# Where the remainder tiles of cosine attention stand, in what order norms and loads come, and how the first weights are split

## The chip, the cores and the metric

The kernel runs on one core of a Trainium2 chip. The metric is the device time of one execution in microseconds (us); shown are a median of three runs and one profiled execution.

## What is computed

Inputs are q, k and v of 8 batches, 12 heads, 448 tokens and 64 elements in f32, the scalar tau, and two weights, `w_in` (768 x 2048) and `w_out` (2048 x 768). The reference, cut:

```python
q_n = q / (norm(q, axis=-1) + 1e-06);  k_n = k / (norm(k, axis=-1) + 1e-06)
attn = softmax(q_n @ k_n.T / tau)              # per batch and head
x = (attn @ v).transpose(0, 2, 1, 3).reshape(8 * 448, 768)
h = x @ w_in
out = maximum(0.01 * h, h) @ w_out             # 3584 x 768, f32
```

## The kernel before

**Attention by pairs of heads.** The 12 heads of a batch make 6 pairs, 48 pairs in all; pair s is pair s % 6 of batch s // 6. `load_qk` (L134) brings a pair's q and k by four DMAs on SyncE's queue into one of six slots of `raw_sb`. `squares` (L170) squares them on GpSimd, `sums` (L183) sums over the 64 elements on VectorE, `roots` (L194) takes the root by Ln and Exp on ScalarE, and `normalise` (L210) divides on VectorE, which gives `qn`. `transposes` (L245) turns `qn` into `qkT`: for pairs 0 to 9 on TensorE and with a copy on VectorE, from pair 10 on (`DMA_FROM`) by one DMA transpose on SyncE's queue. `norm` (L689) is roots, normalise and transposes of one pair, then loads of a later pair, a one-element copy on GpSimd that waits for this pair's `qn` (`hold`, L508), and the squares of a later pair behind it. `ss`, `qn` and `sq` have three buffers each, `qkT` five.

**Scores.** 448 tokens are three key tiles of 128 and a rest of 64. `key_tiles` (L264) computes a tile of keys against all 448 queries of both heads of a pair (L276: two matmuls of 64 rows side by side), then Exp on ScalarE (L288). The rests of two pairs share one remainder tile (ki = 3): eight matmuls in a 64 x 64 arrangement for two tiles, four for one. A batch has 18 key tiles and 3 remainder tiles. `attend_two` and `attend` (L660, L649) form the totals and products with v (L303 for the rests, L316 for the others), the reciprocals on ScalarE (L335, L336) and the scaled result `xT` on VectorE (L357).

**The two matrix products.** Tokens are taken in chunks, by turns of 384 and 512 columns, chunk b with batch b. `first` (L371) computes 128 rows m of h for a chunk: six matmuls over kt (L380), then the leaky ReLU on ScalarE (L387). `firsts` (L707) does all 16 m of a chunk and calls, ahead of given m, the functions of a table (`between`). `groups` (L438) computes one row of 128 tokens of the output in two halves, as 32 steps of two 64-row matmuls side by side (L455), and yields after each step. At the half of a row TensorE waits until the two halves' products have drained. `second` (L406) does the last chunk's rows (L417).

**A visit.** `visit` (L717) goes through the rows of chunk b and lays the 18 key tiles of batch b+1 between their steps: a table says after which steps, one or two at a time (`three` for rows of 384 columns, `four` for 512, `wide` for the first visit, where two rows go together). Two remainder tiles stand at the beginning (L722), the third at the end (L732). `norms` tells which norms of later pairs are called after which steps. Then `attend_batch` (L678), v's loads on GpSimd's queue, and `firsts` of the next chunk. There are seven visits, 0 to 6. All order is written out by hand, engine by engine; each engine runs its instructions in the order in which they are written.

**Banks.** The eight PSUM banks are dealt by `banks` (L75): the ones that were dealt or given back longest ago; a pair of banks for a key tile and for a row of `groups`, one for an m of `first`.

**The beginning.** Before the first visit, batch 0's attention runs pair by pair (`scaled`, L566, and `bulk`, L552, set the loads of v, w_in and further pairs), then the first m of chunk 0. `load_w_in` (L103) loads, by GpSimd's queue, one of four quarters: half of the 2048 columns, and the even or the odd kt. `load_w_out` (L109) loads a quarter of w_out, four m.

## Time and profile before

| | |
|---|---|
| median of three runs | 410.41 us (409.35 to 410.95) |
| profiled execution | 409.29 us, span 407.5 us |
| TensorE (PE) busy | 399.5 us, 98% |
| ScalarE (ACT) busy | 263.0 us, 65% |
| VectorE (DVE) busy | 189.1 us, 46% |
| GpSimd (POOL) busy | 139.5 us, 34% |
| stretch from the start to the first visit | 51.2 us |
| visits 0 and 1 begin at | 51.2 and 98.8 us |

Busy time of TensorE counts matmuls that overlap in its pipeline once; how full it is inside that time is read from the starts of neighbouring instructions. Lines of the views below give start and length in us, engine, line, operation, tiles, shape and count, and in brackets the idle time before and what ended it. A name such as `64*128` behind the tiles is the part of TensorE's array that a matmul takes.

### The profile page before, as it was taken

What the parts mean: (1) busy time and instruction counts of PE and PEld (TensorE: products, weight loads), DVE (VectorE), ACT (ScalarE), POOL (GpSimd) and SP (SyncE); (2) the same over time, 40 slices, a digit from 0 to 9 for tenths busy, and PEclk for the clock granted to TensorE, in tenths of its full rate; (3) what the DMA queues carried; (4) which work ended last, traced back from release to release, by engine and by line L of the source; (5) the groups of instructions that cost most, each with busy time, mean ns of one, the idle gap of its engine ahead of it and who ended that gap; (6) DMA issues with size and microseconds to landing.
All of it is one profiled execution on the core that took longest, in us unless ns stands there. A gap on an engine that the chain in (4) does not pass through costs nothing.

```text
span 407.5 us, 10174 instructions
## 1 busy us (share of the span) xinstructions
PE 399.5 (98%) x4086; PEld 215.8 (53%) x4096; DVE 189.1 (46%) x405; ACT 263.0 (65%) x454; POOL 139.5 (34%) x213
## 2 busy tenths in 40 slices
PE   8889999999999999999999999999999999999996
PEld 3335666544555655544555555544555555554564
DVE  6986941771644624354542635256261645130021
ACT  4996588565865688745876569845876559944300
POOL 4973661571323522253241614055231530000000
PEclk9999999999999999999999999999999999999999
DMA  7999999694496859378384947485478742210033
GB/s 187 252 209 235 194 184 213 196 209 107 117 204 101 146 83 218 63 119 179 78 207 103 137 114 165 110 117 138 93 183 151 103 82 63 63 41 2 0 78 78
DMA packets 102095, 54.21 MB, mean 133 GB/s; under 512 B 69984, under 2 KB 96992, under 8 KB 102048
## 3 DMA queue, kind: packets, MB, share of 16 engines
q1 hardware_dynamic: 78064, 41.04, 43.8%
q0 software_dynamic: 23136, 12.00, 22.5%
q8 instruction: 32, 0.52, 0.5%
q10 hardware_dynamic: 848, 0.52, 0.4%
q14 instruction: 15, 0.12, 0.1%
HBM read 45.61 MB, written 11.01 MB: 139 GB/s over the span
## 4 chain that ended last, share of the span: by engine, by line
PE 87%; DMA 8%; POOL 3%; DVE 1%; issue 0%; ACT 0%; POOLq 0%
PE ps L380 32%; PE ps L455 31%; PE ps L316 10%; PE ps L276 7%; DMA raw_sb<-in_k_dram 5%; PE ps L417 5%; DMA w_in_sb<-in_moe_w_in_dram 2%; POOL sq L179 1%; PE ps L303 1%; POOL v_rem L164 1%; DVE qn L219 0%; POOL v_b L157 0%; POOL raw_sb L129 0%; POOL w_in_sb L105 0%; ACT L65 0%
## 5 line engine op out<-in xcount | busy, mean ns | idle before, releaser
L380 PE MATMUL ps<-xT,w_in_sb 128*128 128x384 bf16 (+1 forms) x760 | 147.8, 352 | 1.0 <-DMA w_in_sb<-in_moe_w_in_dram 0.6
L455 PE MATMUL ps<-w_out_sb,hT 64*128 64x384 bf16 x1536 | 143.5, 323 | 0.0
L288 ACT ACTIVATE pe<-ps 128x896 bf16<-128x896 f32 x144 | 123.6, 918 | 19.9 <-PE ps L276 18.0
L387 ACT ACTIVATE hT<-ps 128x384 bf16<-128x384 f32 (+1 forms) x128 | 67.6, 543 | 71.7 <-PE ps L380 71.3
L380 PEld LDWEIGHTS <-w_in_sb 128*128 128x128 bf16 x768 | 74.1, 98 | 72.4 <-issue 4.0
L455 PEld LDWEIGHTS <-hT 64*128 64x128 bf16 x1536 | 75.0, 94 | 53.9 <-PE ps L455 4.2
L179 POOL TENSOR_TENSOR sq<-raw_sb 128x512 f32<-128x512 f32 x92 | 84.9, 943 | 17.2 <-DMA raw_sb<-in_k_dram 16.3
L219 DVE TENSOR_TENSOR qn<-raw_sb,r 128x512 bf16<-128x512 f32 x96 | 58.0, 646 | 1.9 <-DVE r L215 0.3
L276 PE MATMUL ps<-qkT 64*128 64x448 bf16 (+1 forms) x384 | 55.0, 354 | 1.6 <-DVE qkT L257 0.8
L467 DVE COPY osb<-ps 128x384 f32<-128x384 f32 x41 | 21.2, 553 | 74.0 <-PE ps L455 43.6
L190 DVE TENSOR_REDUCE ss<-sq 128x6 f32<-128x384 f32 (+1 forms) x95 | 54.4, 610 | 1.2 <-POOL sq L179 1.0
L510 POOL CAST seen<-qn 128x1 f32<-128x1 bf16 x47 | 8.7, 186 | 122.0 <-DVE qn L219 121.1
L214 DVE TENSOR_SCALAR ss<-ss 128x14 f32<-128x14 f32 x48 | 9.5, 197 | 69.4 <-ACT ss L198 69.3
L357 DVE TENSOR_TENSOR xT<-ps,rb 128x448 bf16<-128x448 f32 x48 | 27.8, 620 | 27.2 <-ACT rb L336 27.1
L157 POOL DMA_DIRECT2D v_b<-in_v_dram x24 | 18.6, 777 | 54.2 <-PE ps L316 54.2
L316 PE MATMUL ps<-pe,v_b 128*32 128x448 bf16 x576 | 32.0, 353 | 0.0
L276 PEld LDWEIGHTS <-qkT 64*128 64x128 bf16 (+1 forms) x384 | 16.7, 96 | 20.6 <-issue 8.7
L423 DVE COPY osb<-ps 128x384 f32<-128x384 f32 (+1 forms) x9 | 4.6, 513 | 36.6 <-issue 22.6
L316 PEld LDWEIGHTS <-v_b 128*32 128x32 bf16 x576 | 15.1, 97 | 12.0 <-issue 0.6
L288 ACT ACTIVATE pr<-ps 128x896 bf16<-128x896 f32 x24 | 21.3, 920 | 0.2 <-PE ps L276 0.2
L335 ACT ACTIVATE rb<-ps 128x448 f32<-128x448 f32 x24 | 12.9, 537 | 13.1 <-PE ps L316 12.2
L417 PE MATMUL ps<-w_out_sb,hT 128*128 128x384 bf16 (+1 forms) x144 | 21.0, 308 | 0.0
(48 smaller groups left out, 185.0 us busy)
## 6 DMA issues: line engine op xcount, KB each, us to landing
raw_sb<-in_q_dram SPq DMA_DIRECT2D x48, 192.0 KB, 3.6
raw_sb<-in_k_dram SPq DMA_DIRECT2D x46, 192.0 KB, 3.8
out_dram<-osb SPq DMA_DIRECT2D x30, 192.0 KB, 2.8
v_b<-in_v_dram POOLq DMA_DIRECT2D x24, 192.0 KB, 4.8
out_dram<-osb SPq DMA_DIRECT2D x12, 384.0 KB, 3.2
w_in_sb<-in_moe_w_in_dram POOLq DMA_DIRECT2D x4, 768.0 KB, 13.2
w_out_sb<-in_moe_w_out_dram POOLq DMA_DIRECT2D x4, 768.0 KB, 9.6
raw_sb<-in_q_dram SPq DMA_DIRECT2D x43, 32.0 KB, 3.5
```

What stands on the lines that cost most here:

```text
L179: eng.tensor_tensor(sq, x, x, op=ALU.mult)
L190: nc.vector.tensor_reduce(o.rearrange("p (h t) -> p h t", h=2), sqs[s][i], axis=AX.X, op=ALU.add)
L219: scalings[s] = nc.vector.tensor_tensor(qn[s][:, lo:hi], x.rearrange("p h t d -> p t h d"), r[:, r0 : r0 + 2 * nt].rearrange("p (h t) -> p ...
L276: nc.tensor.matmul(out=out[:, a, :S], lhsT=x[rows, c0:c1], rhs=x[rows, 0:S], start=True, stop=True,)
L288: nc.scalar.activation(out=dst, in_=sc[:, :, :S], func=AF.Exp, scale=inv_tau)
L316: nc.tensor.matmul(out=x[32 * g : 32 * g + 32, :S], lhsT=weights(g, ki) if ki < 3 else rem(g), rhs=pe[s][:, ki, a, :] if ki < 3 else pr[j] ...
L357: scalings[j, e] = nc.vector.tensor_tensor(xT[m][:, 2 * jj + e, half * S : (half + 1) * S], pos.pop((j, e))[:, :S], rbs[j], op=ALU.mult,)
L380: nc.tensor.matmul(out=pm[:, :n], lhsT=w_in_sb[:, kt, m * 128 : (m + 1) * 128], rhs=xT[c // 2][:, kt, c0 : c0 + n], start=(kt == 0), stop= ...
L387: nc.scalar.activation(out=hT[c][:, m, :n], in_=pms.pop((c, m))[:, :n], func=AF.Prelu, alpha=0.01)
L417: nc.tensor.matmul(out=po2[:, :n], lhsT=hT[c][:, m, ts * 128 : (ts + 1) * 128], rhs=w_out_sb[:, m, lo : lo + n], start=(m == 0), stop=(m = ...
L455: done[p][i] = nc.tensor.matmul(out=pos2[p][:, i, :HALF], lhsT=hT[c][rows, m, ts * 128 : (ts + 1) * 128], rhs=w_out_sb[rows, m, half * HAL ...
L467: copy(out=osb[c, ts][:, half * HALF : (half + 1) * HALF], in_=po2[:, i, :HALF])
```

## The change

It has four parts. In visits 1 to 6 all three remainder tiles stand at the visit's beginning, and the key tiles' steps are set anew; in visit 0 the last row gets two key tiles at its half and one step less. Pairs are normed earlier, so that all six of a batch are turned before their visit begins; in `firsts` of the odd chunks the norms follow one another without loads, and the loads come together behind them (pairs 12 to 17 behind norm 11); `qkT` gets seven buffers. Around the first visit, pairs 8 to 11 are loaded, squared and normed earlier, and the w_out quarters follow norms 6 to 8. The first half of w_in's columns is loaded in three parts of two neighbouring kt each instead of two parts of three; its second half is loaded as before, both parts at one place.

```diff
-    qtp = ctx.enter_context(tc.tile_pool(name="qt", bufs=5))
+    qtp = ctx.enter_context(tc.tile_pool(name="qt", bufs=7))
...
-    def load_w_in(i):
-        n0, e = i // 2 * (D_ff // 2), i % 2
...
+    def load_w_in(half, j=slice(None), e=slice(None)):
+        n = slice(half * D_ff // 2, (half + 1) * D_ff // 2)
+        gp.dma_start(out=w_in_t[:, j, e, n], in_=w_in_r[:, j, e, n])
...
         if s == 0:
             load_v(1)
-            load_w_in(0)
+            load_w_in(0, j=0)
         elif s == 1:
             load_v_rem(0, slice(2, 4))
-            load_w_in(1)
+            load_w_in(0, j=1)
         elif s == 2:
+            load_w_in(0, j=2)
             load_v(2)
-            load_w_in(2)
         elif s == 3:
-            load_w_in(3)
+            for e in range(2):
+                load_w_in(1, e=e)
...
-        if s in (0, 2):
-            load_qk(7 + s // 2)
+        if s == 0:
+            load_qk(7)
+        elif s == 2:
+            load_qk(8)
+            load_qk(9)
         elif s == 4:
             behind(nc.sync, scalings[5], "weights first")
-            load_qk(9)
+            load_qk(10)
...
+        if s == 4:
+            squares(8)
...
     def attend_batch(b):
         if b == 1:
-            load_qk(14)
-            load_qk(15)
             sums(12)
         attend_two(b * NQ)
-        if b == 1:
-            norm(12)
+        if b % 2:
+            norm(12 if b == 1 else (b + 1) * NPAIR + 1)
...
-    def norm(s, transposed=True):
+    def norm(s, transposed=True, load=True):
...
-        for x in (12, 13) if s == 11 else (s + 4,) if s > 11 else ():
+        for x in range(12, 18) if s == 11 else (s + NPAIR,) if s > 11 and load else ():
             load_qk(x)
...
-        squares(s + 2)
-        if s in (7, 8):
-            load_w_out((4,) if s == 7 else (8, 12))
+        if s not in (9, 17):
+            squares(s + (3 if s < 9 else 2))
+        if s < 9:
+            load_w_out((4 * (s - 5),))
...
-        key_tiles([(s0 + 1, 3), (s0 + 3, 3)])
+        key_tiles([(s0 + 1, 3), (s0 + 3, 3)] + [(s0 + 5, 3)] * (b > 0))
...
-        key_tiles([(s0 + 5, 3)])
+        if b == 0:
+            key_tiles([(s0 + 5, 3)])
...
+    wide = (at(5, 11, 16, 22, 27, 33, 38, 44, 49, 55, 60), at(4, 8, 12, 16, 16, 21, 26))
+    three = (at(9, 16, 16, 21, 26, 31), at(5, 10, 16, 16, 21, 26, 31), at(5, 10, 16, 16, 20))
+    four = (at(9, 16, 16, 24), at(4, 10, 16, 16, 24), at(4, 10, 16, 16, 24), at(5, 10, 16, 16))
...
-            5: [lambda: sums(8), lambda: transposes(6)],
-            7: [lambda: norm(8, False), lambda: transposes(7)],
-            8: [lambda: sums(9)],
-            10: [lambda: norm(9, False), lambda: load_v(3)],
-            11: [lambda: transposes(8), lambda: load_v(4)],
-            13: [lambda: load_v(5), lambda: load_v_rem(1)],
-            14: [lambda: transposes(9), lambda: sums(10)],
+            4: [lambda: norm(8, False)],
+            5: [lambda: transposes(6), lambda: sums(9)],
+            7: [lambda: transposes(7)],
+            8: [lambda: norm(9, False)],
+            10: [lambda: transposes(8), lambda: load_v(3)],
+            11: [lambda: sums(10), lambda: load_v(4)],
+            12: [lambda: transposes(9)],
+            13: [lambda: norm(10), lambda: load_v(5), lambda: load_v_rem(1)],
+            15: [lambda: sums(11)],
...
+        s = (b + 2) * NPAIR
+        if b == 0:
+            norms = {(0, 3): [lambda: norm(11)]}
+        elif b % 2:
             norms = {}
+            for i in range(3):
+                norms[i, 4] = [lambda x=s + i: norm(x)]
+                norms[i, 20] = [lambda x=s + i + 1: sums(x)]
+        else:
+            norms = {(2, 8): [lambda: sums(s + 1)], (2, 22): [lambda: norm(s)]}
...
+        if b % 2:
             between = {
+                0: [lambda: norm(s + 3)], 2: [lambda: sums(s + 4)], 4: [lambda: norm(s + 4)],
+                6: [lambda: sums(s + 5)], 8: [lambda: norm(s + 5)], 12: [lambda: sums(s + 6)],
             }
         else:
+            left = range(s + (2 if b else 1), s + NPAIR)
+            between = {}
+            for x, m in zip(left, (0, 3, 5, 8, 10)):
+                between[m] = [lambda x=x: sums(x), lambda x=x: norm(x, load=False)]
+            between[12] = [lambda x=x: load_qk(x + NPAIR) for x in left]
+            if b == 0:
+                between[12].append(lambda: squares(19))
+            between[14] = [lambda: sums(s + NPAIR)]
```

## The prediction

> **What bounds the kernel now.** I read the page first (busy times, chain), then the instructions of TensorE in order of time, then those of VectorE, GpSimd and SyncE's queue around the places that the edits touch.
>
> ```profile
> span 407.5 us, 10174 instructions
> ...
> PE 87%; DMA 8%; POOL 3%; DVE 1%; issue 0%; ACT 0%; POOLq 0%
> ```
>
> The profiled execution took 409.29 us, its span 407.5; 1.8 us lie around it. The chain that ends last is TensorE's for 87%; the DMA and GpSimd pieces of it all lie before 49 us. So from there on an edit counts only through what it takes out of TensorE's stream or puts in as a wait. In order of time (start, length, engine, line, tiles; the stretch is the visit of chunk 1 with its beginning and end):
>
> ```profile
> 98.84 0.57 PE L276 MATMUL ps<-qkT 64*64 64x448 bf16 x8
> 99.34 0.99 PE L455 MATMUL ps<-w_out_sb,hT 64*128 64x384 bf16 x10
> 100.17 0.35 PE L276 MATMUL ps<-qkT 64*128 64x448 bf16 x2
> 100.35 1.14 PE L455 MATMUL ps<-w_out_sb,hT 64*128 64x384 bf16 x12
> ...
> 120.96 2.76 PE L455 MATMUL ps<-w_out_sb,hT 64*128 64x384 bf16 x32
> 123.65 0.38 PE L276 MATMUL ps<-qkT 64*64 64x448 bf16 x4
> 123.96 0.38 PE L303 MATMUL ps<-pr,ones 64*32 64x448 bf16 x8
> ```
>
> Read starts against starts. Twelve L455 matmuls last 0.98 us (one pair 0.1625), a key tile (L276, 64*128) between them 0.18 to 0.19, and neither leaves a gap: the spreading of the key tiles costs nothing. Only the remainder tiles (L276, 64*64) do: two of them at the beginning take 0.50 for two rounds of 0.19, so 0.12 is a switch of shape; one at the end takes 0.31, again 0.19 and 0.12, and 0.09 before it (120.96 and 16 x 0.1625 is 123.56).
>
> Small losses before that, in the same view:
>
> ```profile
> 29.46 0.34 PE L380 MATMUL ps<-xT,w_in_sb 128*128 128x384 bf16 x1
> 30.38 0.66 PE L380 MATMUL ps<-xT,w_in_sb 128*128 128x384 bf16 x3 [0.59 <-DMA w_in_sb<-in_moe_w_in_dram]
> ...
> 48.54 0.79 PE L233 MATMUL ps<-id,qn 128*128 128x128 bf16 x7
> 49.16 2.11 PE L380 MATMUL ps<-xT,w_in_sb 128*128 128x384 bf16 x12
> ...
> 67.50 0.37 PE L276 MATMUL ps<-qkT 64*128 64x448 bf16 x2
> 67.84 0.83 PE L455 MATMUL ps<-w_out_sb,hT 64*128 64x384 bf16 x8
> ```
>
> First, the second product of w_in waits for the load with the odd kt: 0.92 from start to start instead of 0.16, so 0.76. Second, the transposes of pair 9 take 0.62 instead of the 0.39 of the other pairs (they wait for the norm): 0.23. Third, one key tile at the half of a row takes 0.34 instead of 0.19: 0.15.
>
> **The change part by part**
>
> *w_in by quads.* One load of 512 KB now brings kt 0 and 1, where two of 768 KB did. The four loads of before landed at 24.4, 30.4, 37.4 and 41.8 us (issue and time to landing, load by load). As the queue is backlogged, bytes count: kt 0 and 1 are there by about 22, kt 2 and 3 by 27, kt 4 and 5, after the same bytes as the second load, at 30.4, needed at 35. So -0.76. GpSimd issues five loads instead of four, 0.77 us more, with idle time behind. But the last quarter still lands at 41.8 at the earliest, and its first use, the second matmul of m=8, stands at 42.47, so at 41.7 after the gain. The loads of pairs 9 and 10, now issued 7 to 9 us earlier, share the DMA engines with it and can cost 0.6 more. I give back 0.35 of bounds 0 and 0.76: **-0.4**.
>
> *Norms of pairs 8 to 11 earlier.* Pair 9 was late because its sums ran at 44.69, behind the scaling of pair 8; that norm moves from m=7 to 4, pair 9's from 10 to 8, and their transposes from 11 and 14 to 10 and 12. If pair 9's load, issued 7 us earlier, lands some 2 us earlier than its 41.25, squares and sums follow by 42 and the transposes, at about 45.8, wait no more: **-0.23**; if it lands no earlier, scaling ends at 46.2, +0.2. The w_out load of m 12 to 15 is now behind squares(11): issued at about 52 instead of 50.3, landed 10.0 later in a queue that is full until 60.3; it is needed at 61.2 before and at 60.4 now: +0.1 (0 to 0.6).
>
> *Visit 0.* The last row gets its doubled key tile at the half: **-0.15** (0 at the least, as another stall may take its place).
>
> *Remainder tiles.* In visits 1 to 6 the third stands behind the first two. It costs one round, 0.19, there; at the end 0.31 + 0.09 go, and the direct change from L455 (64*128) to L303 (64*32), which no row shows, comes: between 0 and 0.19 (the change from 64*32 to 128*32 at 124.16, where 16 matmuls of two rounds take 0.57). With the 0.09 that stands before the 64*64 tile: -0.12 a visit, **-0.7** for six (0 to -1.3). [...] All eight banks are now dealt at a visit's beginning: the first row's pair falls to the banks of m=14 and 15, whose L387 runs from 98.94 to 99.54 and would end about when the row starts, at 99.53. I take +0.1 for the three visits after chunks of 512, none for 384. The key tiles that follow (n=9, 16, 16, 21 ...) find their banks free by 0.3 to 0.8 us, with one exp of 0.8 to 0.86 after the other on ScalarE; ScalarE does 21 of them, 17.9 us, in a visit of 19.9.
>
> *The price: all six pairs turned before the visit.* The third remainder tile needs pair s+5's DMA transpose at the visit's beginning. In the even visits after a chunk of 384 the last norm stands at m=8, as one does now: its transpose was issued at 141.49, 3.4 us to landing, so 144.9, needed at 146.6. In visits 3 and 5 I get 1.9 us to spare. In visit 1 five norms, pairs 13 to 17, follow one another. The rows to reckon with, first VectorE, then GpSimd:
>
> ```profile
> 83.95 1.14 DVE L190 TENSOR_REDUCE ss<-sq 128x8 f32<-128x512 f32 x2
> 85.71 0.52 DVE L214 TENSOR_SCALAR ss<-ss 128x14 f32<-128x14 f32 x1 [0.62 <-ACT ss L198]
> 86.27 0.24 DVE L215 RECIPROCAL r<-ss 128x14 f32<-128x14 f32 x1
> 86.54 1.45 DVE L219 TENSOR_TENSOR qn<-raw_sb,r 128x512 bf16<-128x512 f32 x2
> ```
>
> ```profile
> 82.53 2.48 POOL L164 DMA_DIRECT2D v_rem<-in_v_dram  x4
> 84.92 0.27 POOL L510 CAST seen<-qn 128x1 f32<-128x1 bf16 x1
> 85.07 1.90 POOL L179 TENSOR_TENSOR sq<-raw_sb 128x512 f32<-128x512 f32 x2
> ```
>
> A norm is 1.14 of sums, 0.62 for the roots on ScalarE, then 1.6 (nothing else running) to 2.2 (squares beside it) on VectorE. GpSimd issues v's loads until 84.9, so squares(15) ends at 87.0 as squares there do now. From 79.06: sums(13) to 80.2, scaled at 82.5; sums(14) 83.6, scaled 86.2; sums(15), held by squares(15), 87.5, scaled 90.1; sums(16) 91.2, scaled 93.6; sums(17) 94.7, scaled 97.0. The transpose is issued by 97.4, lands 2.9 later (the shortest; no load stands before it): 100.3. The tile wants it at 98.84 + 0.38 = 99.25. So **+1.0** (0 to 2.5: the scaling at 1.6 throughout, or 0.5 more for each of the three that meet squares, as L219 took 2.00 at 46.92 instead of 1.45). ScalarE waits in its queue for these roots meanwhile, with L387 behind; TensorE runs up to eight m ahead, 1.3 us each, and doesn't notice. [...]
>
> Moved past SyncE's queue: pairs 12 to 17 load in one go behind transpose 11 (24 issues, about 14 us from 57), and the first rows' stores come behind them at about 72 instead of 69; three osb buffers cover that. Pairs 19 to 23 stand behind transpose 17, in time for squares(19) at about 103. The seven qkT buffers only lift a wait.
>
> **Sum**: -0.4 - 0.23 + 0.1 - 0.15 - 0.7 + 0.1 + 1.0 = **-0.3 us**: 409.0 for an execution like the profiled one. The three runs' median, 410.41, lies 1.1 above it; I set the forecast against the median: **410.1 us**.
>
> **Rivals**
>
> *Visit 1 not held up.* If VectorE's norms run at 1.6 and GpSimd is free sooner, transpose 17 is in time: -1.3, 409.1. For it: squares overlap only half of the norms. Against: v's loads hold GpSimd until 84.9.
>
> *Visit 1 held up longer.* The three scalings that meet squares take the 0.5 more each: the wait is 2.5, the sum +1.2, 411.6. For it: two rows of L219 near 2.00 (38.38 and 46.92), both beside squares. Against: the scalings at 85.71 and 89.67 beside squares took 1.45 and 1.16.
>
> *A real gain.* In addition the last quarter of w_in isn't waited for and the change from L455 to L303 is free: -0.76 - 0.23 - 0.15 - 1.3 = -2.4, 408.0.
>
> *Slower: ScalarE blocked behind roots(10) and roots(11).* They now stand at m=13 and three steps into visit 0, before L387 of m=13 to 15 and the key tiles' exps. Before, the loads of pairs 10 and 11 landed at 47.4 and 51.3. If they land no earlier, squares(10) end at 49.2, sums at 49.8, roots at 50.4; three L387 follow until 51.9, and the rows of visit 0 want all banks at 50.6: +1.3. Then squares(11) end at 53.2, roots(11) at 54.4, and the key tile at n=16 waits 0.9; w_out's last part, issued behind them at 54, is some 0.5 late. With the sum's -0.3: +2.4, 412.8. It decides from pair 11 landing later than about 50. For it: DMA is full between 10 and 50 us, so an earlier issue may only queue. [...]
>
> *It doesn't do what it says.* The order of the program shows the same 8194 rows on TensorE, the third remainder tile moved in six visits, and the loads as written; left is that kt 1 lands no earlier, which gives back 0.4: 410.5.
>
> **How the numbers follow.** The forecast with its own spread (409.5 to 411.3) has 0.32; visit 1 not held up 0.13; held up longer 0.14; real gain 0.17; ScalarE blocked 0.2; w_in no earlier 0.04. A measurement of this kernel tells about 0.5% (2.05 us) from no change. Faster than that, below 408.36: the real gain and little else, 0.18. Slower, above 412.46: nearly all of ScalarE blocked, and the half of visit 1 held up longer in which a late w_in or w_out comes on top, 0.26. Same: 0.56. The range runs from just below the real gain, 407.8, to just above the price of the slow rival, 413.0; about a tenth is left out on each side.
>
> **What would show it.** Right: no wait at the first L380; 12 L276 of 64*64 at the beginning of visits 1 to 6, 0.69 long; L303 within 0.1 of the end of L455; an idle TensorE of about 1 us only at visit 1, released by the transpose. Wrong: idle time at other visits' beginnings, L276 waiting for the exps of L288 in visit 0, or L380 at m=8 waiting over 0.5 for w_in.

## The result, and the profile after

The changed kernel takes 413.99 us in the median of 19 runs (410.38 to 415.90), the kernel before, on the same chip, 409.82 (408.65 to 411.61, 19 runs): a ratio of 1.0095 (95% interval 1.0076 to 1.0115), 4 us slower. The forecast was 410.1, the range ended at 413.0. The profiled execution took 415.73, 1.7 above the median. Two lines of its page:

```profile
span 413.9 us, 10179 instructions
...
PE 82%; DMA 10%; POOL 3%; DVE 2%; issue 1%; ACT 1%; SPq 0%; POOLq 0%; DVEq 0%
```

The chain ends with less of TensorE and more of DMA than before (82% and 10%, from 87% and 8%). Where that DMA stands is seen in TensorE's order of time, at the beginning and the end of visit 1:

```profile
100.58 1.86 PE L276 MATMUL ps<-qkT 64*64 64x448 bf16 x10
105.09 0.38 PE L276 MATMUL ps<-qkT 64*64 64x448 bf16 x2 [2.65 <-DMA qkT<-qn]
105.40 2.67 PE L455 MATMUL ps<-w_out_sb,hT 64*128 64x384 bf16 x18
...
128.70 2.76 PE L455 MATMUL ps<-w_out_sb,hT 64*128 64x384 bf16 x32
131.39 0.38 PE L303 MATMUL ps<-pr,ones 64*32 64x448 bf16 x8
```

The first ten remainder matmuls should last 0.76 (they do in later runs) and last 1.86: they wait 1.10 for transpose 16. The last two wait 2.65 more for transpose 17. So TensorE stops for 3.75. Then 18 L455 take 2.67, where 18 take 1.64 elsewhere, although nothing holds them. The next view says why: a microsecond to a line, its length, TensorE's busy time and matmuls, the granted clock, the share of DMA and GB/s.

```profile
104.00:105.00 1.00, 0.00 (x0) 1.00 0.71 112
105.00:106.00 1.00, 0.91 (x10) 0.92 0.91 260
106.00:107.00 1.00, 1.00 (x10) 0.50 0.61 173
107.00:108.00 1.00, 1.00 (x10) 0.50 0.69 177
108.00:109.00 1.00, 1.00 (x10) 0.50 0.78 245
109.00:110.00 1.00, 1.00 (x14) 0.87 0.45 78
```

After the stop the granted clock is 0.50, from 105.84 to 109.26 if the two mixed microseconds are split: 3.42 us at half speed, 1.7 lost. Stage by stage, from starts in the two traces (visit: first remainder tile to the first L303; the same stage is read the same way in both):

| stage | before | after | difference |
|---|---|---|---|
| start to visit 0 | 51.21 | 52.53 | +1.32 |
| visit 0 to first L380 of chunk 1 | 26.80 | 27.22 | +0.42 |
| chunk 1's L380 | 20.83 | 20.83 | 0 |
| visit 1 | 25.12 | 30.81 | +5.69 |
| behind visit 1 to the first L380 of chunk 2 | 6.56 | 6.48 | -0.08 |
| from there to the end (visits 2 to 6) | 276.98 | 276.03 | -0.95 |

The loss lies ahead of chunk 2, most of it in visit 1; whether the 1.32 before visit 0 belongs to the change is looked at below. The five visits that follow do what was meant: no wait at their beginning, L303 right behind L455, 0.19 each.

**Why transpose 17 is late.** VectorE at the norms of pairs 14 to 17 (L219 is the scaling), then GpSimd beside that of pair 14, then SyncE's queue:

```profile
85.87 0.86 DVE L214 TENSOR_SCALAR ss<-ss 128x14 f32<-128x14 f32 x1 [0.62 <-ACT ss L198]
...
87.03 2.48 DVE L219 TENSOR_TENSOR qn<-raw_sb,r 128x512 bf16<-128x512 f32 x2
...
97.27 1.16 DVE L219 TENSOR_TENSOR qn<-raw_sb,r 128x512 bf16<-128x512 f32 x2 [1.65 <-DMA qkT<-qn]
...
100.92 1.16 DVE L219 TENSOR_TENSOR qn<-raw_sb,r 128x512 bf16<-128x512 f32 x2
```

```profile
84.19 2.48 POOL L164 DMA_DIRECT2D v_rem<-in_v_dram  x4
...
86.74 2.36 POOL L179 TENSOR_TENSOR sq<-raw_sb 128x512 f32<-128x512 f32 x2
```

```profile
82.27 3.52 SPq L251 DMA_TRANSPOSE qkT<-qn  x1
85.89 0.98 SPq L139 DMA_DIRECT2D raw_sb<-in_q_dram  x1
...
88.86 14.51 SPq L251 DMA_TRANSPOSE qkT<-qn  x5
```

The scaling of pair 16 waits 1.65 for a transpose: there are three `qn` buffers, and pair 16 takes that of pair 13. Pair 13 was scaled at 84.1, but its transpose, the first of the five in the last line, was issued only at 88.86: ahead of it in the queue were the 24 loads of pairs 12 to 17 (59.3 to 80.5), three stores, transpose 12 and the four loads of pair 18. It landed 8.3 later. In the profile before, pair 13's transpose was issued as its scaling ended, and most of these transposes landed 2.9 to 3.1 later:

```profile
84.10 1.26 SPq L251 DMA_TRANSPOSE qkT<-qn  x1
```

Scaling 17 ends at 102.0, transpose 17 is issued at 102.15 and lands 2.9 later, at 105.05.

In the beginning the forecast gain is there and is given back at once:

```profile
29.37 0.82 PE L380 MATMUL ps<-xT,w_in_sb 128*128 128x384 bf16 x4
...
33.87 0.75 PE L316 MATMUL ps<-pe,v_b 128*32 128x448 bf16 x12 [0.69 <-DMA v_b<-in_v_dram]
...
42.98 1.31 PE L380 MATMUL ps<-xT,w_in_sb 128*128 128x384 bf16 x7 [0.31 <-DMA w_in_sb<-in_moe_w_in_dram]
...
48.36 0.34 PE L233 MATMUL ps<-id,qn 128*128 128x128 bf16 x3 [0.70 <-DVE qn L219]
...
56.75 0.37 PE L276 MATMUL ps<-qkT 64*128 64x448 bf16 x2 [0.42 <-ACT pe L288]
```

The first L380 wait for nothing (0.76 gained), but v(2), now one place further back in GpSimd's queue, is waited for (0.69), then the last quarter of w_in (0.31). Pair 9's load now lands early (at 36.5, before at 41.25), but its scaling falls together with the squares of pair 10, and TensorE waits 0.70 for it:

```profile
45.62 2.27 POOL L179 TENSOR_TENSOR sq<-raw_sb 128x512 f32<-128x512 f32 x2 [3.94 <-DMA raw_sb<-in_k_dram]
```

```profile
45.65 2.65 DVE L219 TENSOR_TENSOR qn<-raw_sb,r 128x512 bf16<-128x512 f32 x2
```

In visit 0 the exps stand behind pair 11's roots.

### The profile page after: what moved, and what is told of

The parts are those of the page before. It is cut to its first block, busy times and chain, and to the rows that moved or that the text cites. A ratio compares the mean times of both kernels' runs of the same rounds, so it can differ in the third digit from the quotient of the medians.

```text
span 413.9 us, 10179 instructions
## 1 busy us (share of the span) xinstructions
PE 402.2 (97%) x4096; PEld 227.1 (55%) x4096; DVE 199.6 (48%) x405; ACT 261.9 (63%) x454; POOL 141.7 (34%) x214
## 4 chain that ended last, share of the span: by engine, by line
PE 82%; DMA 10%; POOL 3%; DVE 2%; issue 1%; ACT 1%; SPq 0%; POOLq 0%; DVEq 0%
PE ps L455 30%; PE ps L380 29%; PE ps L316 10%; PE ps L276 7%; PE ps L417 5%; DMA raw_sb<-in_k_dram 5%; DMA v_b<-in_v_dram 3%; DMA qkT<-qn 3%; POOL sq L179 2%; PE ps L303 1%; DVE qn L219 1%; POOL v_rem L164 1%; DVE ss L190 0%; POOL raw_sb L129 0%; POOL w_in_sb L107 0%
## 5 line engine op out<-in xcount | busy, mean ns | idle before, releaser
L380 PE MATMUL ps<-xT,w_in_sb 128*128 128x384 bf16 (+1 forms) x768 | 148.0, 353 | 0.3 <-DMA w_in_sb<-in_moe_w_in_dram 0.3
L455 PE MATMUL ps<-w_out_sb,hT 64*128 64x384 bf16 x1536 | 145.8, 325 | 0.0
L288 ACT ACTIVATE pe<-ps 128x896 bf16<-128x896 f32 x144 | 124.8, 918 | 21.2 <-PE ps L276 19.9
L380 PEld LDWEIGHTS <-w_in_sb 128*128 128x128 bf16 x768 | 74.0, 98 | 72.1 <-issue 3.7
L455 PEld LDWEIGHTS <-hT 64*128 64x128 bf16 x1536 | 86.1, 95 | 44.4 <-PE ps L455 4.4
L387 ACT ACTIVATE hT<-ps 128x384 bf16<-128x384 f32 (+1 forms) x128 | 65.4, 542 | 48.9 <-PE ps L380 48.2
L179 POOL TENSOR_TENSOR sq<-raw_sb 128x512 f32<-128x512 f32 x92 | 86.7, 964 | 27.1 <-DMA raw_sb<-in_k_dram 26.1
L467 DVE COPY osb<-ps 128x384 f32<-128x384 f32 x41 | 21.2, 553 | 95.9 <-PE ps L455 59.2
L219 DVE TENSOR_TENSOR qn<-raw_sb,r 128x512 bf16<-128x512 f32 x96 | 63.2, 700 | 3.6 <-DMA qkT<-qn 1.6
L276 PE MATMUL ps<-qkT 64*128 64x448 bf16 (+1 forms) x384 | 56.2, 354 | 4.8 <-DMA qkT<-qn 2.7
L214 DVE TENSOR_SCALAR ss<-ss 128x14 f32<-128x14 f32 x48 | 14.0, 292 | 49.5 <-ACT ss L198 49.4
L197 ACT ACTIVATE ss<-ss,tiny 128x14 f32<-128x14 f32 x48 | 14.6, 304 | 31.4 <-DVE ss L190 31.1
L276 PEld LDWEIGHTS <-qkT 64*128 64x128 bf16 (+1 forms) x384 | 18.4, 97 | 22.3 <-issue 9.2
```

The source lines that it names most:

```text
L179: eng.tensor_tensor(sq, x, x, op=ALU.mult)
L219: scalings[s] = nc.vector.tensor_tensor(qn[s][:, lo:hi], x.rearrange("p h t d -> p t h d"), r[:, r0 : r0 + 2 * nt].rearrange("p (h t) -> p ...
L276: nc.tensor.matmul(out=out[:, a, :S], lhsT=x[rows, c0:c1], rhs=x[rows, 0:S], start=True, stop=True,)
L288: nc.scalar.activation(out=dst, in_=sc[:, :, :S], func=AF.Exp, scale=inv_tau)
L380: nc.tensor.matmul(out=pm[:, :n], lhsT=w_in_sb[:, kt, m * 128 : (m + 1) * 128], rhs=xT[c // 2][:, kt, c0 : c0 + n], start=(kt == 0), stop= ...
L387: nc.scalar.activation(out=hT[c][:, m, :n], in_=pms.pop((c, m))[:, :n], func=AF.Prelu, alpha=0.01)
```

## The experiments

Theory A: the loss is visit 1's hold-up, by SyncE's queue and the `qn` buffers, and the clock that falls behind it. Rivals: another place for the loss (B, C), other causes of the stop (G), no cost of the clock. The kernel before, run beside each group of kernels, took 409.23, 409.48, 409.56, 409.84 and 409.47 us (medians of 17 to 29 runs); times below are medians, ratios are to the kernel before beside it.

### Where: the third tile in visit 1, or the beginning

```diff
-        key_tiles([(s0 + 1, 3), (s0 + 3, 3)] + [(s0 + 5, 3)] * (b > 0))
+        key_tiles([(s0 + 1, 3), (s0 + 3, 3)] + [(s0 + 5, 3)] * (b > 1))
...
-        if b == 0:
+        if b < 2:
             key_tiles([(s0 + 5, 3)])
```

> The changed kernel with one thing undone: in visit 1 the third remainder tile stands at the end again. Theory A (visit 1 is held up at its beginning for pair 17's transpose, and TensorE's clock falls behind the wait): the wait of 4.1 us and the slow matmuls behind it, 1.7, are gone; left are the slower beginning, +1.7, and 0.2 less in each of visits 2 to 6: about 0.7 us over the kernel before (ratio 1.002, 410.5 us). Rival B (the wait only moves, to the tile at the visit's end or to the key tiles of pairs 16 and 17): at most 1 us better than the changed kernel, 413.

Measured: 409.22 us, ratio 0.9996 (0.9981 to 1.0011). Visit 1 is 25.13 long, as before the change, and its end has the old form again:

```profile
99.26 0.57 PE L276 MATMUL ps<-qkT 64*64 64x448 bf16 x8
...
121.38 2.76 PE L455 MATMUL ps<-w_out_sb,hT 64*128 64x384 bf16 x32
124.08 0.38 PE L276 MATMUL ps<-qkT 64*64 64x448 bf16 x4
124.39 0.38 PE L303 MATMUL ps<-pr,ones 64*32 64x448 bf16 x8
```

One tile of four matmuls, 25 us later in one visit, takes 4.2 us off the changed kernel by the ratios to the kernel before (4.8 by the medians, which come from different groups of runs). The time lies below the 410.5 that was expected, because the late beginning that this took over from the changed kernel's trace isn't there in the median. The opposite experiment, the old beginning with the tile left in front (all edits of w_in, of `scaled` and of the norms of pairs 8 to 11 undone, of which a few lines):

```diff
-            load_w_in(0, j=2)
             load_v(2)
+            load_w_in(2)
...
-            4: [lambda: norm(8, False)],
-            5: [lambda: transposes(6), lambda: sums(9)],
+            5: [lambda: sums(8), lambda: transposes(6)],
+            7: [lambda: norm(8, False), lambda: transposes(7)],
```

> The changed kernel with the beginning of the kernel before: w_in by halves, loads and norms of pairs 8 to 11 where they were; the visits and the firsts from chunk 1 on as changed. Theory A: the beginning and visit 0 lose their 1.7 us, visit 1 still waits about 4 us: 412.3. Rival C (the late beginning is what makes visit 1 late, as its loads of pairs 12 to 17 start later): the wait of visit 1 falls to about the 1.0 us forecast, with no fall of the clock: 409.5.

413.92 us, ratio 1.0104 (1.0072 to 1.0136): as the changed kernel, and above the 412.3 expected for the same reason. TensorE's last stop at visit 1 is 2.62. The late beginning is not what makes transpose 17 late.

### Why TensorE stops, and what the clock costs

```diff
-    qnp = ctx.enter_context(tc.tile_pool(name="qn", bufs=3))
+    qnp = ctx.enter_context(tc.tile_pool(name="qn", bufs=5))
```

> The changed kernel with five qn buffers in place of three. If the scaling of pair 16 waits for the transpose of pair 13 to give its buffer back (1.65 us in the profile), the transpose of pair 17 lands 1.6 us earlier, visit 1 waits 2.5 instead of 4.1 us, and the clock falls for a shorter time or not at all: 2 to 3.3 us less than the changed kernel, about 411.5. If VectorE and GpSimd alone pace the five norms, no change.

412.3 us, ratio 1.0061 (1.0038 to 1.0083). The wait of L219 is gone, the ten matmuls last 0.76, and of the stop this is left:

```profile
104.08 0.38 PE L276 MATMUL ps<-qkT 64*64 64x448 bf16 x2 [2.07 <-DMA qkT<-qn]
```

So 3.75 became 2.07, and the time fell by 1.7 by the medians, 1.4 by the ratios, about the buffer's wait. The clock still falls, for 3.40 us. This execution also has a wait in visit 0 that the changed kernel's trace doesn't have, the one for w_out which the forecast put at 0.1 (0 to 0.6):

```profile
63.77 0.34 PE L455 MATMUL ps<-w_out_sb,hT 64*128 64x384 bf16 x2 [1.08 <-DMA w_out_sb<-in_moe_w_out_dram]
```

(Where an edit adds lines, the numbers of later lines move: L281, L460, L385 and L308 are L276, L455, L380 and L303 of the others.)

Next, 14 matmuls of ones into the third tile's bank ahead of it in visit 1, work that the kernel doesn't need, so that TensorE doesn't stand idle:

```diff
             tiles.append(sc)
+            if busy and (s, ki) == which[-1]:
+                for x in range(busy):
+                    nc.tensor.matmul(
+                        out=sc[:, 0], lhsT=warm[:, :128], rhs=warm, start=(x == 0), stop=(x == busy - 1)
+                    )
```

> The changed kernel, with 14 matmuls of 512 columns on a constant tile (3.0 us) ahead of the third remainder tile of visit 1, into the bank that this tile then overwrites; results are the same. If the clock falls because TensorE stands idle, it stays at 1.0, the matmuls behind the wait run at 0.163 a pair instead of 0.27, and the time falls by about 1.7 us at an equal wait (412.3). If the clock falls for another reason (the load after it, the chip's own beat), nothing changes, or the time rises a little.

412.24 us, ratio 1.007 (1.0043 to 1.0097), against 413.99:

```profile
98.94 0.57 PE L281 MATMUL ps<-qkT 64*64 64x448 bf16 x8
99.44 3.19 PE L272 MATMUL ps<-warm 128*128 128x512 bf16 x13
102.57 0.38 PE L281 MATMUL ps<-qkT 64*64 64x448 bf16 x4
```

In the records are 13 of the 14. The granted clock is 1.00 throughout, and the visit's first 18 L455 run at full rate. Filling the wait with useless work takes 1.7 us off the changed kernel by the medians and 1.0 by the ratios, which is of the size of the lost clock. In this execution transpose 17 was there when the filling ended, so the fill itself set the visit's 28.26.

### Which idle time costs the clock

On the kernel with the tile last in visit 1, TensorE is made to wait in visits 2 to 6: a matmul of ones, 1, 3, 5, 7 and 9 copies on VectorE one after the other, a matmul of the copy.

```diff
+            if busy and (s, ki) == which[-1]:
+                nc.tensor.matmul(out=sc[:, 0], lhsT=warm[:, :128], rhs=warm, start=True, stop=True)
+                for x in range(busy):
+                    nc.vector.tensor_copy(cold, sc[:, 0])
+                nc.tensor.matmul(out=sc[:, 0], lhsT=cold[:, :128], rhs=cold, start=True, stop=True)
```

> The kernel with the third tile of visit 1 at its end, and in visits 2 to 6 TensorE is made to stand idle ahead of the third remainder tile: one matmul of ones into the tile's bank, 1, 3, 5, 7 and 9 copies of it by VectorE one after the other, and a matmul of the copy. Theory I (TensorE's granted clock falls because TensorE stood idle for over some 1 to 2 us): the clock stays 1.00 behind the shortest idle and falls to about 0.5 for some 3 us behind the long ones. Rival J (it fell in visit 1 for another reason, DMA or all engines busy at once): it stays 1.00 behind all five. Each copy should take about 0.6 us.

The five stops were 1.11, 2.78, 4.01, 5.67 and 7.12 us. The shortest and the next:

```profile
149.17 0.38 PE L281 MATMUL ps<-qkT 64*64 64x448 bf16 x4 [1.11 <-DVE cold L273]
```

```profile
199.57 0.59 PE L281 MATMUL ps<-qkT 64*64 64x448 bf16 x4 [2.78 <-DMA raw_sb<-in_q_dram]
```

(VectorE's three copies end at 198.98; the name in the second bracket is the latest event, not the cause. The matmul of the copy is missing from the records: only its weight load shows, so TensorE stood idle less than each stop is long, by an estimate some 0.3 to 0.5, as L501's matmuls of the same 128x512 mostly last 0.38 in the profile before, and 0.63 at the most.) In the views by microseconds, the first behind the stop of 1.11, the second behind that of 2.78, the third behind that of 4.01 (the last two with all engines: TensorE, its weight loads, VectorE, ScalarE and GpSimd, then the clock):

```profile
149.00:150.00 1.00, 0.83 (x12) 1.00 0.00 0
```

```profile
198.00:199.00 1.00, 0.00 (x0) 0.00 (x0) 0.94 (x2) 0.22 (x1) 0.00 (x0) 0.99 0.92 297
199.00:200.00 1.00, 0.43 (x4) 0.24 (x5) 0.00 (x0) 0.00 (x0) 0.00 (x0) 0.50 0.45 83
200.00:201.00 1.00, 1.00 (x10) 0.43 (x8) 0.00 (x0) 0.79 (x1) 0.00 (x0) 0.50 0.93 284
201.00:202.00 1.00, 1.00 (x10) 0.46 (x8) 0.36 (x2) 0.54 (x3) 0.00 (x0) 0.50 0.52 138
202.00:203.00 1.00, 1.00 (x12) 0.57 (x10) 0.97 (x3) 0.00 (x0) 0.00 (x0) 0.80 0.67 156
```

```profile
253.00:254.00 1.00, 1.00 (x12) 0.58 (x14) 0.00 (x0) 0.92 (x1) 0.00 (x0) 0.80 0.00 0
254.00:255.00 1.00, 1.00 (x10) 0.49 (x8) 0.00 (x0) 0.00 (x0) 0.00 (x0) 0.50 0.00 0
```

The clock falls to 0.50 in or behind all stops but the shortest, 1.11. In the third view, as in the stop ahead of it, DMA moves nothing, and the stops stand in five visits, so neither DMA nor the place in the program makes it fall; standing idle does. From 198.98 to 202.40 it is 3.42 us long.

### Is SyncE's queue the cause?

The loads were spread: only pairs 12 to 15 behind transpose 11, pair 16 behind transpose 12, pair 17 behind transpose 13, pair 18 at m=12.

```diff
-        for x in range(12, 18) if s == 11 else (s + NPAIR,) if s > 11 and load else ():
+        for x in range(12, 16) if s == 11 else (s + 4,) if s < 14 else (s + NPAIR,) if load else ():
...
+                between[12].insert(0, lambda: load_qk(18))
+                between[12].append(lambda: squares(18))
```

> The changed kernel, with SyncE's queue put in another order: behind transpose 11 only pairs 12 to 15 are loaded, pair 16 behind transpose 12, pair 17 behind transpose 13, pair 18 with the others at m=12. Theory A says that transpose 13 sat behind 24 loads, three stores, a transpose and a load (issued at 88.9, its pair normalised at 84.1), and that so the scaling of pair 16 waited 1.65 for pair 13's qn buffer: transpose 13 is then issued near 84.5 and the wait at L219 goes; transpose 17 lands 1.5 to 2 earlier, the stop of TensorE at visit 1 shrinks from 2.65 to about 1 and the clock is lost for less time or not at all; the time 1.5 to 3.5 below the changed kernel, 410.5 to 412.5. Rival G (GpSimd's squares and the scalings beside them set it, not the queue): the wait goes over to squares or scalings, visit 1 stays over 29.5, the time over 412.5.

421.37 us, ratio 1.0289 (1.0255 to 1.0324). This edit does more than it says: its condition also holds for norms 6 to 9, which load pairs 10 to 13 a second time. So it tells nothing of theory A, but it shows a rival of the forecast at work, ScalarE blocked behind roots:

```profile
56.20 0.59 PE L276 MATMUL ps<-qkT 64*64 64x448 bf16 x4 [5.03 <-ACT ss L198]
```

Squares and sums came late, roots stood in ScalarE's queue, and L387 and the exps behind them. Mended (`s in (12, 13)` and `s > 11`):

> The kernel of the loads spread, mended: that one also loaded pairs 10 to 13 a second time, behind norms 6 to 9. Here only pairs 12 to 15 load behind transpose 11, pair 16 behind transpose 12, pair 17 behind transpose 13, pair 18 at m=12. Theory A (SyncE's queue holds transpose 13 and so pair 13's qn buffer): transpose 13 issued near 84.5, no wait of L219 for qn, TensorE's stop at visit 1 about 1 instead of 2.65, 410.5 to 412.5. Rival G (squares and scalings set it): visit 1 over 29.5 long and the time over 412.5.

412.72 us, ratio 1.0076 (1.0052 to 1.0100). Transpose 13 is issued at 83.76, and L219 waits for nothing. At visit 1:

```profile
102.61 0.38 PE L276 MATMUL ps<-qkT 64*64 64x448 bf16 x2 [1.78 <-DMA qkT<-qn]
...
109.18 0.36 PE L276 MATMUL ps<-qkT 64*128 64x448 bf16 x2 [1.62 <-ACT pe L288]
```

The stop went from 3.75 to 1.78 with the clock at 1.00: the queue's part is shown. But a new stop of 1.62 has come: pair 18's load is now late, its sums end at 107.7, and its roots stand in ScalarE's queue ahead of the exps. The same with five `qn` buffers:

> The same with five qn buffers. Theory A: as five buffers alone took 1.7 us off the changed kernel and spreading the loads lets the transposes go early, both together take off no more than the larger of the two, since each removes the same wait: 410.5 to 412. If two waits in series were there, it is 409.5 or less.

413.55 us, ratio 1.009 (1.0062 to 1.0118); the stop is again 1.78, the second one 2.19, the clock 1.00. More buffers and a freer queue remove one and the same wait, as theory A said. The size forecast for it, 410.5 to 412, was missed by the second stop.

Then pair 18 loads behind transpose 14 (`(s + 4,) if s in (12, 13, 14)`, and squares where they were):

> The loads spread as in the mended kernel, but pair 18 loads behind transpose 14 instead of at m=12, so that its roots don't stand late ahead of the exps. Theory A, split in two: the queue of SyncE made the stop at visit 1 longer (3.75 in two pieces in the changed kernel, 1.78 here) and so brought the fall of the clock; the chain of norms keeps 1.78. Expected: stop 1.8 at visit 1, clock 1.00 behind it, no second stop; the time 1.6 below the mended kernel, 411.1 (410.5 to 411.8). Rival K (the earlier load delays the transposes again): the stop 2.5 or more and the clock lost, 412.5 or more.

412.49 us, ratio 1.0056 (1.0031 to 1.0082), where 411.1 was expected. The second stop is gone, but the squares of pairs 16 and 17 now wait 0.57 and 0.72 for their loads, and the stop is

```profile
103.57 0.38 PE L276 MATMUL ps<-qkT 64*64 64x448 bf16 x2 [2.36 <-DMA qkT<-qn]
```

That is half of rival K. In this execution the clock stayed at 1.00 behind 2.36 of idle (the last section shows where that stop lies); over the seven runs the mean clock was 0.999 or 1.0 in three (410.2 to 412.5 us) and 0.995 or 0.996 in four (411.9 to 414.2).

Last, the chain of norms shortened: the sums of pair s+1 between roots and scaling of pair s, squares one pair further ahead.

```diff
         roots(s)
+        if early:
+            sums(early)
         normalise(s)
...
+        if s == 12:
+            squares(14)
-        if s not in (9, 17):
-            squares(s + (3 if s < 9 else 2))
+        if s not in (9, 16, 17):
+            squares(s + (3 if s < 9 or 11 < s < 16 else 2))
```

> The first kernel of this call, and the chain of norms made shorter: the sums of pair s+1 stand between the roots and the scaling of pair s, so that VectorE doesn't wait 0.62 for ScalarE's roots, and the squares run one pair further ahead (pair 15's before v's loads on GpSimd). Theory A (what is left of the stop is the chain of five norms, 3.66 each): scaling 17 ends some 2 us earlier, the stop at visit 1 is under 0.5, the time 409 to 410. Rival G (GpSimd's squares set it): scaling 17 no earlier than in the first kernel, the stop stays near 1.8.

415.23 us, ratio 1.0129 (1.0106 to 1.0151): theory A fails here. GpSimd's queue:

```profile
96.42 1.82 POOL L179 TENSOR_TENSOR sq<-raw_sb 128x512 f32<-128x512 f32 x2 [6.71 <-DMA raw_sb<-in_k_dram]
```

Pair 17's loads were issued from 85.35 to 88.4 and are there at 96.4. Spread loads let the transposes go early and bring the squares late; loads in one go do the reverse. With one queue for both, none of the arrangements tried has transpose 17 in time.

### The beginning

Three kernels with the third tile last in visit 1: the whole beginning as before, only w_in as before, only loads and norms of pairs 8 to 11 as before. The edits are those of the two kernels of the first part, put together in these ways.

> The beginning as before, and the third remainder tile of visit 1 at its end; of the change the five other visits' remainder tiles are left, and the last norms turned without loads between. From the traces each of these visits is 0.2 us shorter with the change (0.08 at the end, 0.12 in the body), so -1.0 for five. Theory A (the late beginning and visit 1's wait are all that the change loses): 1.0 below the kernel before, ratio 0.9975, the span 0.5 to 1.5 shorter than that of the third-tile-last kernel with the new beginning, the visit of chunk 0 starting near 51.2. Rival D (the new beginning is no loss of its own, its 1.3 us in the trace being drift from run to run): no shorter than that kernel, ratio 0.9995.

> The third remainder tile of visit 1 at its end, and w_in loaded as before; the loads and norms of pairs 8 to 11 stay early. Theory E (the quads put v(2)'s load one place back and lengthen the backlog, so that the loads after them are late): the visit of chunk 0 starts near 51.2, the 0.69 waits for v(2) and for w_in at m=8 go, the wait of 0.59 at the second product comes back. Rival F (the early raw loads of pairs 8 to 10 take the DMA engines from v(2) and w_in): the visit of chunk 0 starts no earlier than 52, the two waits stay.

> The third remainder tile of visit 1 at its end, and the raw loads and norms of pairs 8 to 11 as before; w_in stays in quads. Theory E (the quads make v(2) and the second half late): the visit of chunk 0 starts near 52, v(2) waited for. Rival F (the early raw loads do): it starts near 50.5, since the second product waits for nothing and the later loads are as early as before; ratio to the kernel before about 0.996.

410.18, 409.54 and 410.01 us, ratios 1.0012 (0.9991 to 1.0033), 1.0009 (0.9991 to 1.0027) and 1.0005 (0.9986 to 1.0025): all the same, none as expected. Visit 0 started at 52.27, 50.45 and 50.31 in the three traces, while with one and the same changed beginning it starts at 50.55 to 52.55 in others. One trace can't tell 1 us there. Visit 0 starts at 51.5 in the mean of ten traces with the changed beginning and at 51.4 in that of six with the old one, so the +1.32 of the table is not shown to be the change's. The first and the third have a new stop, though the tile stands last:

```profile
100.66 1.35 PE L276 MATMUL ps<-qkT 64*64 64x448 bf16 x7 [0.27 <-ACT hT L387]
```

Visit 1 takes 26.76 and 27.23 there instead of 25.13. The first kernel's trace shows the chain: scaling 15 waits 2.43, until transpose 12, issued at 82.96, has landed 10.5 later; so the norms behind it are late, roots 17 run at 99.57, and six L387 stand behind them on ScalarE until 102.9, whose banks the remainder tiles want. The queue's lateness reaches the visit by a second way.

### A version without the price

Nearly the kernel before up to visit 2 (the new steps of the key tiles and the seven `qkT` buffers stay), third tile first and norms without loads between only from visit 3 on (norm 24 in visit 2, loads of 28 to 30 behind it):

```diff
+        key_tiles([(s0 + 1, 3), (s0 + 3, 3)] + [(s0 + 5, 3)] * (b > 2))
...
+        if b < 3:
             key_tiles([(s0 + 5, 3)])
...
+        for x in (12, 13) if s == 11 else (s + 4,) if 11 < s < 24 else (28, 29, 30) if s == 24 else (s + NPAIR,) if s > 24 and load else ():
```

> The kernel before up to the end of visit 2, with its loads, norms and third tiles last; from visit 3 on as the changed kernel (third tile first, last norms without loads between). Theory A (each visit from the second on gains 0.2 and pays nothing): 0.8 below the kernel before, ratio 0.998, no wait in visits 3 to 6. Rival H (the norms without loads between cost in every batch something that the stage lengths of TensorE don't show): ratio 1.000 or more.

410.69 us, ratio 1.0024 (1.0008 to 1.0039), slower, by one wait behind visit 2:

```profile
167.55 0.38 PE L303 MATMUL ps<-pr,v_rem 64*32 64x448 bf16 x7 [1.28 <-DVE osb L467]
```

VectorE holds norm 24 there, which waited 4.12 for its roots, ahead of the row's copy out of the bank. So norm 24 to the fourth step:

```diff
-                (1, 20): [lambda: sums(24)], (2, 8): [lambda: sums(25)], (2, 22): [lambda: norm(24)],
+                (1, 20): [lambda: sums(24)], (2, 4): [lambda: norm(24)], (2, 20): [lambda: sums(25)],
```

> As the kernel with only visits 3 to 6 changed, but norm 24 stands at the fourth step of the last row of visit 2 instead of the 22nd, so that its scaling isn't ahead of the row's copy to osb when its roots come late. Theory A: the wait of 1.28 at L303 goes and the four visits' gain is left: 0.8 below the kernel before, ratio 0.998. Rival H (the norms without loads cost something elsewhere): ratio 1.000 or more without a wait in visits 2 to 6.

408.89 us, ratio 0.9973 (0.9957 to 0.9989): as expected, and 1.1 us faster than the kernel before. TensorE has no wait from visit 0 on, and visit 0 takes 20.09 from its first tile to its first L303, where the kernel before takes 20.22. Run again, beside its twin with the new beginning:

> The twin with the old beginning, run again beside it on the same chip. By the four visits' gain of 0.2 each it is 0.8 below the kernel before, ratio 0.998; the first time it was 0.9973 (0.9957 to 0.9989).

> The kernel that is faster than the one before (only visits 3 to 6 changed, mended), with the changed beginning: w_in's first half by quads, loads and norms of pairs 8 to 11 earlier. By the forecast's own terms (-0.4 for w_in, -0.23 for pair 9's transposes, +0.1 for w_out) it is 0.5 below its twin with the old beginning. Theory L (the gain at the second product is given back where v, the second half of w_in and pair 11 land later): the twin or up to 1 above it, ratio 0.997 to 1.000.

408.51 us, ratio 0.9984 (0.9965 to 1.0003), and 409.16, ratio 0.9996 (0.9982 to 1.0009). The second time the interval takes in 1, so the gain over the kernel before is clear once and not twice; against the changed kernel it is clear both times. The means of the twelve runs are 408.93 and 409.07, 0.14 apart, with an interval of some 0.9 to either side: the new beginning is worth nothing that this measurement can tell, and neither the forecast gain nor a small loss is excluded.

## Why the prediction was wrong, point by point

**The step that failed is the price of turning all six pairs before visit 1**, +1.0 (0 to 2.5) in the sum; it is 5.9 in the profile (the visit's 5.69 and the 0.2 that it gains like the others), and 4.4 to 5 by the runs with and without the tile in front (4.2 by the ratios, 4.8 by the medians, and the 0.2). The mechanism, VectorE's chain of norms and the transpose behind it, was right, but it was a part of the price only. By the forecast's timetable the tile waits 1.05 for transpose 17; in the profile it could start at about 101.0 and the transpose lands at 105.05, so 4.06. Of the 3.0 more, 1.65 is a wait for a buffer and 1.6 is pair 14's scaling, less 0.3 elsewhere; 1.7 of the clock comes on top. The terms that were missing or too small:
- *The queue and the buffers.* The forecast timed only the last transpose ("no load stands before it", true: it landed in 2.9) and no earlier one, and it put the issues of the 24 loads at about 14 us from 57. They took 21.2, from 59.3 to 80.5. So transpose 13, behind 28 loads, three stores and a transpose, held `qn`'s third buffer: 1.65. Five buffers, or loads spread, take this wait away.
- *Scaling beside squares.* 0.5 more for a scaling that meets squares was the upper bound; pair 14 took 3.64 on VectorE behind its roots, where the forecast has 2.0 on average: L214 and L219 took 3.34, where 1.33 is the least (0.17 and 1.16). L214's 0.86 stands beside GpSimd's issues of v's loads, before the squares begin, and is 0.7 of it. L219's 2.48 stands beside squares, and is 1.3. Where both of a scaling's operations meet squares it takes 2.48 to 2.65 (38.51, 45.65 and 87.03). The forecast's rows for a smaller price were others: at 38.38 and 46.92 the squares began 0.24 and 0.48 after the scaling (2.00), at 86.54 they ended 0.4 behind its start (1.45), and at 90.40 they had ended (1.16). So in these rows a scaling lasts the longer, the longer squares stand beside it, and up to 1.5 more than alone (2.65 to 1.16); a pair's two squares last 1.82 alone (96.42 in the last kernel with spread loads) and 2.27 to 2.36 beside the scalings at 38.51, 45.65 and 87.03. No run takes the squares away from the scalings, so this part is read from rows and not tested.
- *The clock.* 1.7 behind the stop. Before, TensorE stood idle for over 1.5 us only at the kernel's end, where a fall of the clock costs nothing; the fall was not among the forecast's terms or bounds at all.

**ScalarE waiting for roots.** "TensorE runs up to eight m ahead, 1.3 us each, and doesn't notice" holds only until the banks are dealt to the remainder tiles; the kernels with loads as before lose 1.6 to 2.1 to it. As a rival at visit 0 its condition came true (pair 11's load landed at 52.7, later than 50), but it cost 0.42 here and 0.6 to 1.6 in other kernels with this beginning; 5.03 where loads are doubled.

**Remainder tiles.** -0.12 a visit forecast, -0.19 measured (276.98 to 276.03 over five). All three in front last 0.76 to the last end, 0.69 by starts. The change from L455 to L303 is the 0.09 that is seen between 128.70 plus 16 x 0.1625 and 131.39. L303's own block became 0.08 shorter (6.56 to 6.48), a term that the forecast didn't have. So it is in part luck that the bound of -1.3 for six was nearly right: six times 0.19 is -1.1.

**The beginning.** -0.4 and -0.23 forecast, no gain that can be told measured. The second product's 0.76 is gained; v(2), moved behind a third load, gives back 0.69, w_in 0.31, and pair 9's scaling, though its load came earlier, met pair 10's squares and gives back 0.70. **Visit 0's key tile**, -0.15, came true where no wait comes on top: -0.13 in the kernels of the last part.

**The sign and the range.** "Visit 1 held up longer" was the nearest rival: the right place, but 411.6. The slow one that was priced highest (412.8) was another place. The changed kernel with its tile last in visit 1 is at 409.2, inside the range, so this one step carries the time out of it. It isn't the only error: without the step's +1.0 the forecast lies 1.3 below the kernel before, and this kernel at best 0.8 below; the 0.6 of the beginning isn't there.

## What to carry to other kernels

A step moved ahead of a deadline must be timed through every buffer ring that its predecessors use: the operation that was late here waited for a buffer held by a transfer three pairs earlier, behind loads that nobody was waiting for yet. In a queue with one order, what is needed last for the next stage (loads) and what is needed first (transposes) can't be moved apart without looking at both. And where the bound engine is near 100% (98% busy here), one long stop can cost more than its length: in the executions with a trace TensorE also lost half of the next 3.4 us behind stops of 2.07 and 2.65 us, and not behind those of 1.78 and 2.36.

## What was not expected of the hardware

TensorE's granted clock fell to 0.50 behind idle stretches of 2.07, 2.15, 2.34, 2.62, 2.65, 2.78 us and more, for 3.40 to 3.42 us, and for longer in stops of 5.03, 5.67 and 7.12 (at least 6.1, 5.6 and 7.6 us in the views), and stayed at 1.00 behind 1.11, 1.78, 2.19 and 2.36. The two lists overlap: not only the length decides, but also where the stop falls. In a trace the changes of the clock that the views show lie on one grid. In the kernel with five stops the clock falls at 198.98 and 253.60 and is back at 202.40, 257.02, 311.62 and 369.66: 54.62 between the falls, 54.62, 54.60 and 58.04 between the returns, which are 16, 16, 16 and 17 times 3.41 us, the length of a single fall. In the changed kernel's trace it falls at 105.84 and, behind the last matmul, at 413.04, which are 307.20 apart, 90 times 3.413. Let TensorE's idle time be summed in the step of the grid that ends where the clock falls: it is 2.65 in the changed kernel, 2.07 with five `qn` buffers, 2.09 with the old beginning, 2.15 and 2.14 at the last two falls with the loads doubled, and 2.19 at the first of the two falls with five stops. A step with 1.60 (five stops, up to 250.19) had no fall at its end. At 0.50 already, the clock stayed there behind a step with 1.30 (loads doubled, 54.90 to 58.31). The stop of 2.36 (101.21 to 103.57) lies across a line of the grid. At the end of its trace the clock falls at 409.73:

```profile
409.00:410.00 1.00, 0.00 (x0) 0.00 (x0) 0.00 (x0) 0.00 (x0) 0.00 (x0) 0.87 0.13 34
```

Counted back from there by 90 steps, 307.20, a line of the grid stands at 102.53, so the stop has 1.32 in one step and 1.04 in the next. Equal kernels ran with and without the fall: of the changed kernel's 19 single runs, two with a mean clock of 0.999 took 410.4 and 410.8, nine with 0.995 took 412.2 to 415.7, four with 0.991 or 0.992 415.3 to 415.9, and the other four, with 0.994 and 0.998, 412.1 to 414.2. One fall of 3.4 us to half clock is 0.4% of 412, so these would be, by that estimate, none, one and two falls; the one execution with a trace has one.

In the changed kernel's trace a DMA transpose took 2.9 us to land with no load ahead of it in SyncE's queue (issued at 98.5 and 102.1) and 7.7 to 9.5 behind loads (82.3, 88.9 and 90.2), and its issue 3.52 (82.27) instead of 1.3.
